# Fused attention and gated feed-forward on one core: first-phase banks, the start of the loop and the last block's outputs rearranged

## The chip, the cores and the metric

The kernel runs on 1 core of one Trainium2 chip. The metric is the device time of one execution in microseconds, as the median of several runs. Every run also reports the span of the core (some 1.8 us less than the time) and the mean clock granted to TensorE. A difference of 2% would count as faster or slower.

## The reference

```python
def mab(q, kv):
    s = scale * (q @ kv.transpose(0, 2, 1))
    a = softmax(s)
    return a @ kv
h = mab(I, x)            # 32 inducing points look at 12416 tokens, 4 batches
x = mab(x, h)            # every token looks at the 32 results
out = (relu(x @ w_gate) * (x @ w_val)) @ w_out      # 49664 tokens, 128 -> 1536 -> 128
```

## The kernel before

Batch 0 has a first phase of its own: cast x, transpose it on TensorE, scores `s1`, exp `p1`, denominators `z1`, and `hT`, the 32 results. The products `hgv` of `hT` with the weights follow in three parts of 512 columns. Then comes the loop that fills the rest of the time. A unit of it is: TensorE forms a gate (two banks of 512) and a value (one tile of two banks), ScalarE takes the relu of the gate, VectorE multiplies the relu with the value into `gv`, and TensorE contracts `gv` with `wo`. The kernel splits PSUM, the memory that TensorE's results go to, into eight banks (3 + 2 x 2 + 1): a ring `g` of three, two two-bank tiles `v`, one bank `o`.

```python
def bank(tag, name, shape=None, dtype=FP32):
    return psum.tile(shape or [P, BLK], dtype, tag=tag, bufs={"g": 3, "v": 2, "o": 1}[tag], name=name)
...
# first phase, batch 0
z1_ps = bank("v", "z1_ps", [P, 2 * BLK])
z1a, z1 = z1_ps[:, 0 : 8 * M], z1_ps[:, BLK : BLK + M]
s1_ps = bank("v", "s1_ps", [P, 2, 2 * TPB, 2 * M])      # scores: one tile of two banks
...
        ps = s1_ps[:, j % 2, :, 0:M]
        for t in range(t0, t1):
            nc.tensor.matmul(ps[:, t - t0, :], xTs(xT, t, 1), indT, start=True, stop=True)
        nc.scalar.activation(out=p1[...], in_=ps[...], func=AF.Exp, scale=sm_scale)
...
# start of the loop: all three parts of hgv first
ps = hgv_pe(hT, 0)
for a in (0, BLK // 2):
    nc.vector.tensor_copy(out=hgv[:, a : a + BLK // 2], in_=ps[:, a : a + BLK // 2])
ps = bank("v", "hgv_ps", [P, 2 * BLK])
for k in (1, 2):
    hgv_pe(hT, k, ps[:, (k - 1) * BLK : k * BLK])
nc.vector.tensor_copy(out=hgv[:, BLK : 2 * BLK], in_=ps[:, 0:BLK])
nc.scalar.copy(out=hgv[:, 2 * BLK : DFF], in_=ps[:, BLK : 2 * BLK])
...
# the last block, its evacuation
for a in (0, h):                                          # h = 2 of 4 token tiles
    nc.vector.tensor_tensor(out=osb[:, a : a + h, :], in0=c["ps"][:, a : a + h, :],
                            in1=zz[0][...], op=ALU.mult)
    nc.sync.dma_start(out=ov[...], in_=osb[:, a : a + h, :])
```

A slot is the place of one unit in the loop. In the first ten slots two filler matmuls a slot keep TensorE busy (`idle`).

The softmax here doesn't subtract the row's maximum and nothing guards it: scores larger than these inputs give would overflow.

## Time and profile before

| | before |
|---|---|
| time, median of 3 runs | 710.46 us (709.27 to 711.6) |
| span of the profiled run | 709.0 us |
| VectorE busy | 678.9 us (96%) |
| ScalarE busy | 675.3 us (95%) |
| first product of the loop | 28.65 us |
| seventh product instruction (the first unit is split in two) | 36.23 us |
| end of the last product | 704.17 us |

Two engines are busy nearly all the time, so the page shows the bound, but not what the ends cost. For that one reads the timeline, line by line: start, length, engine, source line, operation, output and inputs, how many instructions are merged in the line, and in brackets how long the engine was idle before it and what ended the idle time. The prediction below shows these lines.

### The profile page before, as it was taken

How to read it: one execution, taken by the hardware profiler on the slowest of the kernel's cores; microseconds unless marked ns; L12 is line 12 of the kernel's file. 1: busy time of each engine (PE TensorE's matmuls, PEld its weight loads, DVE VectorE, ACT ScalarE, POOL GpSimd, SP SyncE). 2: the span in 40 equal slices, each digit the busy share in tenths (PEclk: the TensorE clock that was granted, in tenths of full speed). 3: DMA queues.
4: the chain of work that ended last, by engine and by line, in shares of the span. 5: the costliest groups of instructions: out<-in, count | busy, mean ns of one | idle time of the engine just before them, and what ended most of it. 6: DMA issues, size and time to landing. Idle time of an engine off the chain costs nothing.

```text
span 709.0 us, 14077 instructions
## 1 busy us (share of the span) xinstructions
PE 637.9 (90%) x4626; PEld 186.0 (26%) x4626; DVE 678.9 (96%) x621; ACT 675.3 (95%) x1382; POOL 350.5 (49%) x646
## 2 busy tenths in 40 slices
PE   6899999999998999999998899999999898888997
PEld 5322222222222222222222222222222222222224
DVE  4599999999999999999999999999999999999997
ACT  5699999999999999999999999999999999999995
POOL 3661637535176546355256362852616443534543
PEclk9999999999999999999999999999999999999999
DMA  8657865431247867523139677653223132231222
GB/s 342 216 129 163 171 178 152 119 82 61 74 145 152 203 167 199 133 82 91 46 107 197 166 175 172 160 124 76 68 67 94 50 90 56 79 89 49 71 58 89
DMA packets 142346, 87.58 MB, mean 124 GB/s; under 512 B 117152, under 2 KB 125632, under 8 KB 139968
## 3 DMA queue, kind: packets, MB, share of 16 engines
q1 hardware_dynamic: 142272, 86.68, 47.2%
q8 instruction: 36, 0.59, 0.4%
q14 instruction: 38, 0.31, 0.1%
HBM read 27.80 MB, written 25.43 MB: 75 GB/s over the span
## 4 chain that ended last, share of the span: by engine, by line
ACT 32%; PE 29%; issue 17%; DVE 14%; DMA 6%; POOL 1%; SPq 1%; ACTq 0%; DVEq 0%
ACT g L961 23%; DVE gv L966 13%; PE o_ps L662 13%; PE v_ps L864 9%; ACT oT L668 5%; PE g_ps L864 4%; DMA gv<-in_x_dram 2%; ACT p2q L195 2%; DMA x<-in_moe_w_val_dram 1%; ACT p1T L527 1%; DMA out_dram<-osb 1%; DMA x<-in_x_dram 1%; PE h_ps L579 1%; POOL osb L679 0%; PE idle_ps L263 0%
## 5 line engine op out<-in xcount | busy, mean ns | idle before, releaser
L966 DVE TENSOR_TENSOR gv<-g,v_ps 128x1024 f16<-128x1024 f16 (+1 forms) x578 | 658.0, 1210 | 9.4 <-PE g_ps L864 5.9
L961 ACT ACTIVATE g<-g_ps 128x512 f16<-128x512 f32 x1164 | 604.0, 618 | 12.3 <-PE g_ps L864 8.5
L662 PE MATMUL o_ps<-gv,wo 128*128 128x512 f16 x1128 | 352.5, 384 | 43.9 <-ACT oT L668 43.9
L679 POOL TENSOR_SCALAR osb<-o,z2i 128x128 f32<-128x128 f16 x380 | 165.9, 453 | 276.0 <-DMA o<-oT 273.9
L864 PE MATMUL g_ps<-p,hgv 32*128 32x512 f16 x1152 | 284.4, 380 | 2.6 <-ACT g L961 1.9
L864 PE MATMUL v_ps<-p,hgv 32*128 32x512 f16 x1152 | 224.2, 384 | 9.5 <-DVE gv L966 7.9
L864 PEld LDWEIGHTS <-hgv 32*128 32x128 f16 x2400 | 69.5, 91 | 269.3 <-issue 264.7
L662 PEld LDWEIGHTS <-wo 128*128 128x128 f16 x1176 | 80.9, 97 | 211.8 <-issue 195.4
L435 POOL TENSOR_TENSOR z2i<-zt,minus 128x16 f32<-128x16 f32 (+3 forms) x31 | 73.2, 2366 | 0.3
L668 ACT CAST oT<-o_ps 128x512 f16<-128x512 f32 (+1 forms) x98 | 58.4, 596 | 0.0
L496 POOL CAST x<-x 128x2048 f16<-128x2048 f32 x18 | 34.0, 1890 | 18.3 <-DMA x<-in_x_dram 18.3
L428 POOL TENSOR_TENSOR zt<-zt 128x32 f32<-128x32 f32 (+5 forms) x124 | 35.1, 283 | 9.7
L428 POOL TENSOR_TENSOR zt<-p2T 128x256 f32<-128x256 f16 (+3 forms) x31 | 17.4, 563 | 25.9 <-DMA p2T<-p 15.2
L270 DVE COPY xT<-xT_ps 128x1024 f16<-128x1024 f16 (+1 forms) x13 | 8.4, 650 | 10.0 <-PE xT_ps L269 9.2
L269 PE MATMUL xT_ps<-eye,x 128*128 128x128 f16 x97 | 9.0, 242 | 5.5 <-POOL x L281 4.8
L282 ACT CAST x<-gv 128x512 f16<-128x512 f32 (+1 forms) x12 | 7.2, 597 | 6.9 <-DMA gv<-in_x_dram 6.9
L195 ACT ACTIVATE p2q<-s_ps 128x512 f16<-128x512 f32 x22 | 13.4, 610 | 0.0
L281 POOL CAST x<-gv 128x512 f16<-128x512 f32 (+1 forms) x12 | 7.2, 598 | 10.2 <-DMA gv<-in_x_dram 10.1
L527 ACT ACTIVATE p1T<-s1T_ps 128x512 f16<-128x512 f32 x18 | 11.1, 616 | 0.0
L179 PE MATMUL s_ps<-xT,hT 128*32 128x512 f16 x108 | 10.8, 392 | 0.2
L601 POOL TENSOR_TENSOR hp<-hp,hq 128x129 f32<-128x129 f32 (+1 forms) x18 | 8.3, 461 | 2.8 <-ACT hq L600 2.8
L966 DVE TENSOR_TENSOR gvr<-g,v_ps 128x512 f16<-128x512 f16 x12 | 8.0, 684 | 1.7 <-PE g_ps L864 1.7
(93 smaller groups left out, 159.1 us busy)
## 6 DMA issues: line engine op xcount, KB each, us to landing
out_dram<-osb SPq DMA_DIRECT2D x95, 256.0 KB, 2.2
x<-in_x_dram SPq DMA_DIRECT2D x18, 1024.0 KB, 6.0
gv<-in_x_dram SPq DMA_DIRECT2D x11, 512.0 KB, 7.5
p<-p2q SPq DMA_DIRECT2D x88, 64.0 KB, 2.0
o<-oT SPq DMA_TRANSPOSE x98, 2.3
x<-in_moe_w_out_dram SPq DMA_DIRECT2D x1, 768.0 KB, 9.2
gv<-in_x_dram SPq DMA_DIRECT2D x2, 256.0 KB, 10.5
x<-in_moe_w_gate_dram SPq DMA_DIRECT2D x1, 512.0 KB, 9.0
```

The costliest lines, as they stand in the source:

```text
L179: nc.tensor.matmul(ps[32 * r : 32 * r + 32, :], hT[:, 0:M], xTs(xT, blocks[r] * TPB, TPB), start=True, stop=True,)
L195: nc.scalar.activation(out=p2q, in_=ps, func=AF.Exp, scale=sm_scale)
L428: nc.gpsimd.tensor_tensor(out=dst, in0=v[:, :, :, 0:m], in1=v[:, :, :, m : 2 * m], op=ALU.add)
L435: nc.gpsimd.tensor_tensor(out=z2i, in0=v[:, :, :, 0], in1=minus1[:, 0 : n * g].rearrange("p (n g) -> p n g", n=n), op=ALU.pow,)
L496: nc.gpsimd.tensor_copy(out=s["x16"][:, t0:t1, :], in_=s["x32", q])
L527: nc.scalar.activation(out=p1T, in_=ps, func=AF.Exp, scale=sm_scale)
L662: nc.tensor.matmul(c["ps"][:, 0:w], wo[:, i, :], gv(i), start=(i == 0), stop=(i == NFF - 1))
L668: nc.scalar.copy(out=oT[:, 0:w], in_=c["ps"][:, 0:w])
L679: nc.gpsimd.tensor_scalar(out=osb[:, t, :], in0=o16[:, t, :], scalar1=zz, scalar2=zz, op0=ALU.mult, op1=ALU.mult,)
L864: nc.tensor.matmul(ps[:, cols], hgv[:, s * P : (s + 1) * P], p2, start=True, stop=True)
L961: nc.scalar.activation(out=g16[:, k * BLK : (k + 1) * BLK], in_=ps, func=AF.Relu)
L966: nc.vector.tensor_tensor(out=ready["dst"][:, a : a + w], in0=ready["g16"][:, a : a + w], in1=ready["v"][:, a : a + w], op=ALU.mult,)
```

## The change

Three intentions. In the first phase the scores of each part take a bank of the ring, so that a tile of two banks is free for the fillers, and the denominators are summed ahead of `hT`. The second and third part of `hgv` become jobs inside the loop, after units 1 and 4, so the loop starts with the first part only; two score jobs of batch 0 move to later slots. The last block's outputs take two banks of the gate ring (384 and 128 columns), scaled by VectorE and ScalarE at once and stored from two queues.

```diff
-    z1_ps = bank("v", "z1_ps", [P, 2 * BLK])
-    z1a, z1 = z1_ps[:, 0 : 8 * M], z1_ps[:, BLK : BLK + M]
-    s1_ps = bank("v", "s1_ps", [P, 2, 2 * TPB, 2 * M])
+    z1a_ps = bank("v", "z1a_ps", [P, 2 * BLK])
+    z1a, idle_ps = z1a_ps[:, 0 : 8 * M], z1a_ps[:, BLK : 2 * BLK]
+    z1 = bank("v", "z1_ps", [P, M])
...
-            ps = s1_ps[:, j % 2, :, 0:M]
+            ps = bank("g", "s1_ps", [P, 8, M])
...
-    ps = bank("v", "hgv_ps", [P, 2 * BLK])
-    for k in (1, 2):
-        hgv_pe(hT, k, ps[:, (k - 1) * BLK : k * BLK])
-    nc.vector.tensor_copy(out=hgv[:, BLK : 2 * BLK], in_=ps[:, 0:BLK])
-    nc.scalar.copy(out=hgv[:, 2 * BLK : DFF], in_=ps[:, BLK : 2 * BLK])
+    idle(idle_ps, 3, xT[0][:, 0:4, :].rearrange("p t c -> p (t c)"))
...
+    ev_hgv(0, 1, 1, 1)          # TensorE, then ScalarE one slot later
+    ev_hgv(0, 2, 4, 4)
...
-                    ev_s2_quad(b, qd, a + 4, a + 8)
+                    ev_s2_quad(b, qd, a + (4 if a else 12), a + (8 if a else 18))
-                ev_s2(b, (b, 1), (2, 3, 2, 3), 5, 8)
+                ev_s2(b, (b, 1), (2, 3, 2, 3), 7, 8)
...
-                ps = bank("o", "o_ps")
+                c["ps"] = bank("g" if last else "o", "o_ps", [P, n, P])      # n = 3 if last
+                if last:
+                    c["ps1"] = bank("g", "o_ps", [P, 1, P])
...
-                for a in (0, h):
-                    nc.vector.tensor_tensor(... half ...);  nc.sync.dma_start(... half ...)
+                nc.vector.tensor_tensor(out=osb[:, 0:n, :], in0=c["ps"], in1=zz[0][...], op=ALU.mult)
+                nc.sync.dma_start(out=ov[...][:, t0 : t0 + n, :], in_=osb[:, 0:n, :])
+                nc.scalar.activation(out=osb1[:, 0, :], in_=c["ps1"][:, 0, :], func=AF.Copy, scale=zz[0][:, n, :])
+                nc.scalar.dma_start(out=ov[...][:, t0 + n : t0 + TPB, :], in_=osb1)
...
-                        job(steps, evac, ([1, 3, 3, 3, 3] if k == 0 else [0] + [4] * 8,) * 2)
+                        job(steps, evac, ([1, 3, 3, 3, 3] if k == 0 else [5] * 8,) * 2)
```

More of the change, by code (lines that the diff above doesn't have):

```diff
@@ L307 @@
                 )
+            end = j == n_parts + 2
+            for t in range(n if j - 3 >= n_big else 0):
+                first, last = j - 3 == n_big and t == 0, end and t == n - 1
+                nc.tensor.matmul(z1, ones16, p1[:, t, :], start=first, stop=last)
             for t in range(n):
-                first, last = j == 3 and t == 0, j == n_parts + 2 and t == n - 1
-                if j - 3 >= n_big:
-                    nc.tensor.matmul(
-                        z1, ones16, p1[:, t, :], start=j - 3 == n_big and t == 0, stop=last
-                    )
+                first, last = j == 3 and t == 0, end and t == n - 1
                 nc.tensor.matmul(hT_ps, x16[:, t0 + t, :], p1[:, t, :], start=first, stop=last)
@@ L319 @@
         if j == n_parts:
-            idle_ps = bank("g", "idle_ps")
             z1s = st([P, M], FP32, "z1s", 1)
@@ L456, in job, with ev_hgv, pe @@
         jobs.append(dict(steps=steps, evac=evac, counts=counts))
+    def ev_hgv(b, k, first, last):
+        def pe(at):
+            ps = hgv_pe(state[b]["hT"], k)
+            post[at + 1].append(lambda: hgv_evac(state[b]["hgv"], ps, k))
+        fill(first, last, pe)
+    ev_hgv(0, 1, 1, 1)
+    ev_hgv(0, 2, 4, 4)
     for b in range(B):
@@ L641, in act @@
                 for k in range(3):
-                    def mk(at, k=k):
-                        ps = hgv_pe(s["hT"], k)
-                        post[at + 1].append(lambda: hgv_evac(s["hgv"], ps, k))
-                    fill(at + 2, at + 9 + 3 * k, mk)
+                    ev_hgv(b, k, at + 2, at + 9 + 3 * k)
             post[at + 1].append(act)
@@ L719, in step @@
             if i == 0:
-                ps = bank("o", "o_ps")
-                nc.tensor.matmul(ps, zero16, wo[0:1, 0:TPB, :], start=True, stop=False)
-                c["ps"] = ps.rearrange("p (t c) -> p t c", t=TPB)
+                n = TPB - 1 if last else TPB
+                c["ps"] = bank("g" if last else "o", "o_ps", [P, n, P])
+                nc.tensor.matmul(c["ps"], zero16, wo[0:1, 0:n, :], start=True, stop=False)
+                if last:
+                    c["ps1"] = bank("g", "o_ps", [P, 1, P])
             for t in range(TPB):
+                alone = last and t == TPB - 1
                 nc.tensor.matmul(
-                    c["ps"][:, t, :],
+                    c["ps1"][:, 0, :] if alone else c["ps"][:, t, :],
                     gv(i)[:, t * P : (t + 1) * P],
                     wo[:, i, :],
-                    start=False,
-                    stop=(i == NFF - 1 and t == TPB - 1),
+                    start=alone and i == 0,
+                    stop=i == NFF - 1 and (alone or t == c["ps"].shape[1] - 1),
                 )
@@ L735, in evac @@
             if last:
-                h = TPB // 2
-                for a in (0, h):
-                    nc.vector.tensor_tensor(
-                        out=osb[:, a : a + h, :],
-                        in0=c["ps"][:, a : a + h, :],
-                        in1=zz[0][:, a : a + h, :].broadcast_to([P, h, P]),
-                        op=ALU.mult,
-                    )
-                    nc.sync.dma_start(
-                        out=ov[key[0]][:, t0 + a : t0 + a + h, :], in_=osb[:, a : a + h, :]
-                    )
+                n = TPB - 1
+                nc.vector.tensor_tensor(
+                    out=osb[:, 0:n, :],
+                    in0=c["ps"],
+                    in1=zz[0][:, 0:n, :].broadcast_to([P, n, P]),
+                    op=ALU.mult,
+                )
+                nc.sync.dma_start(out=ov[key[0]][:, t0 : t0 + n, :], in_=osb[:, 0:n, :])
+                osb1 = st([P, 1, P], FP32, "osb1", 1)
+                nc.scalar.activation(
+                    out=osb1[:, 0, :], in_=c["ps1"][:, 0, :], func=AF.Copy, scale=zz[0][:, n, :]
+                )
+                nc.scalar.dma_start(out=ov[key[0]][:, t0 + n : t0 + TPB, :], in_=osb1)
                 return
```

## The prediction

That a smaller idle gap of TensorE makes the full clock likelier rests on the one stretch at 0.50 in the trace before (29.79 to 33.20 us), after that gap. That a second queue is worth one issue at most rests on issues of 0.33 to 0.39 us. For the 0.15 us of the wider last store no working is given; the page of the kernel before has 1.7 us from issue to landing for stores of 128 KB and 2.2 for 256 KB.

> **What bounds the kernel now.** I read the busy shares first, then the costliest groups, then the timeline of the two ends, because the diff only touches the ends.
>
> From the page of the kernel before (engine busy times; then group: engine, operation, tile, shapes, count | busy us, mean ns | idle before):
>
> ```profile
> PE 637.9 (90%) x4626; PEld 186.0 (26%) x4626; DVE 678.9 (96%) x621; ACT 675.3 (95%) x1382; POOL 350.5 (49%) x646
> ...
> L966 DVE TENSOR_TENSOR gv<-g,v_ps 128x1024 f16<-128x1024 f16 (+1 forms) x578 | 658.0, 1210 | 9.4 <-PE g_ps L864 5.9
> L961 ACT ACTIVATE g<-g_ps 128x512 f16<-128x512 f32 x1164 | 604.0, 618 | 12.3 <-PE g_ps L864 8.5
> ```
>
> VectorE's product gate times value is 658 of 709 us and sits idle only 9.4 us in all. ScalarE (relu 604, plus chain copies, plus exps) is almost as full. So the long middle is a VectorE/ScalarE bound with nothing to give: a change that leaves the instructions of the loop alone can win only before the loop is at full pace and after its last product. The timeline of the start:
>
> ```profile
> 27.47 0.59 ACT L339 CAST hgv<-hgv_ps 128x512 f16<-128x512 f32 x1 [1.40 <-DVE hgv L338]
> 27.95 3.05 ACT L961 ACTIVATE g<-g_ps 128x512 f16<-128x512 f32 x6
> 28.61 0.37 PE L864 MATMUL g_ps<-p,hgv 32*128 32x512 f16 x1 [1.36 <-ACT g L961]
> 28.65 1.29 DVE L966 TENSOR_TENSOR gv<-g,v_ps 128x512 f16<-128x512 f16 x2 [1.21 <-POOL wo L885]
> 30.16 1.22 DVE L966 TENSOR_TENSOR gv<-g,v_ps 128x1024 f16<-128x1024 f16 x1 [0.23 <-PE v_ps L864]
> 31.74 1.22 DVE L966 TENSOR_TENSOR gv<-g,v_ps 128x1024 f16<-128x1024 f16 x1 [0.35 <-PE v_ps L864]
> 33.25 1.22 DVE L966 TENSOR_TENSOR gv<-g,v_ps 128x1024 f16<-128x1024 f16 x1 [0.29 <-PE v_ps L864]
> 34.76 1.22 DVE L966 TENSOR_TENSOR gv<-g,v_ps 128x1024 f16<-128x1024 f16 x1 [0.29 <-ACT p2q L195]
> 36.23 20.71 DVE L966 TENSOR_TENSOR gv<-g,v_ps 128x1024 f16<-128x1024 f16 x18 [0.25 <-ACT p L190]
> ```
>
> ScalarE's first relu waits behind its copy of the last third of hgv, which waits for VectorE's copy of the second third. TensorE, whose three gate banks are full, idles 1.36 us at 28.61. Then five products start 1.5 us apart (30.16, 31.74, 33.25, 34.76, 36.23) where the full pace is 20.71/18 = 1.15. The stretches show why (columns: stretch, its length, busy us and count of PE, PEld, DVE, ACT, POOL, then the granted TensorE clock, DMA share, GB/s):
>
> ```profile
> 29.00:30.00 1.00, 1.00 (x7) 0.23 (x8) 0.93 (x2) 1.00 (x4) 0.77 (x4) 0.89 0.61 188
> 30.00:31.00 1.00, 1.00 (x9) 0.16 (x6) 0.84 (x1) 1.00 (x3) 0.84 (x3) 0.50 1.02 426
> 31.00:32.00 1.00, 1.00 (x7) 0.19 (x6) 0.65 (x2) 0.42 (x2) 1.00 (x1) 0.50 0.78 328
> 32.00:33.00 1.00, 1.00 (x6) 0.11 (x4) 0.96 (x1) 0.67 (x2) 0.22 (x2) 0.50 0.06 16
> 33.00:34.00 1.00, 1.00 (x11) 0.28 (x8) 0.75 (x1) 0.90 (x2) 1.00 (x1) 0.90 0.00 0
> ```
>
> After the idle gap the clock falls to half for about 3.4 us (0.22 us of the first row, three whole rows, 0.2 us of the last), TensorE is busy all of it, and products wait for v_ps. The end:
>
> ```profile
> 701.90 0.39 PE L864 MATMUL v_ps<-p,hgv 32*128 32x512 f16 x2 [0.58 <-DVE gv L966]
> ...
> 702.44 2.85 PE L724 MATMUL o_ps<-wo,gv 128*128 128x128 f16 x48
> 705.38 0.76 DVE L738 TENSOR_TENSOR osb<-o_ps,zz 128x256 f32<-128x256 f32 x2 [1.21 <-issue]
> 705.84 0.81 SPq L744 DMA_DIRECT2D out_dram<-osb  x2
> ```
>
> The last product ends at 704.17 (the chain of waits: 703.58 + 0.60), but the 48 output matmuls could begin only when the single output bank had been copied away (ScalarE's copy, 701.49 + 0.59), so TensorE runs until 702.44 + 2.85 = 705.29. Then two VectorE halves in a row and two stores, the second issued at 706.3 (the groups of the output tensor), landing some 1.7 us later.
>
> [...] The trace's issues cost 0.33 to 0.39 us against 1.7 us to landing, so a second queue is worth one issue at most. [...] The trace gives 420 ns for 256 columns and 691 ns for a 512-column cast, so about 1.06 ns per column.
>
> **The change, part by part.**
>
> *End of the first phase.* The 32-column scores no longer share one two-bank tile; each takes a bank of the ring of three. Before, the score matmuls of 22.40 waited for ScalarE's exp of the part before (end 22.34), and the two exps after it stand at 22.75 and 23.42, 0.67 us apart, because score and exp alternate. After, the instruction order shows no ScalarE wait on those matmuls: they can go at about 22.05, the next exps at about 22.35 and 23.05. The softmax denominators are also summed ahead of hT, so the reciprocal (356 ns) partly hides. Gain **about 0.4 us** at hT.
>
> *Head of the loop.* The copies of the second and third parts of hgv leave the path and become ScalarE jobs after units 1 and 4. VectorE loses one copy (0.69 us); ScalarE gains one. The first relu now waits only for the first gate matmuls: hgv's first part is there at about 26.1, three filler matmuls (0.65 us at 0.216 each) end at 26.35, gates at about 26.45, relu 26.85 to 27.4, first product about 27.45; less the 0.4 above, **27.05 instead of 28.65, 1.6 us earlier**. On the way to full pace the new order carries two ScalarE copies (0.5 us each in a back-to-back stream) but two exps (0.6 each) move from units 4 to 6 to units 8 to 13, where ScalarE's relus run ahead (20 in 9.93 us, 0.99 a unit, against VectorE's 1.15). If the clock stays full, I walk units 0 to 5 at ScalarE's pace: relus of units 0, 1, copy, 2, 3, 4, copy, 5 are 12 x 0.51 + 2 x 0.5 = 7.1 us from 26.85 - 0.4 = 26.45, so the sixth product starts near 33.5 to 34.2 instead of 36.23: **2.0 to 2.7**, less some 0.3 when the moved exps come due: 2.0. If the clock still drops (0.36 us lost in each of 3 to 4 units) it is about 0.9. TensorE's 1.36 us gap shrinks to a few tenths, so I give the full clock 70%: 0.7 x 2.0 + 0.3 x 0.9 = **1.7 us**.
>
> *The tail.* With two gate banks, free once unit 11's relus have been read (about 701.1), 20 of the 48 matmuls go before the last values, 28 after. The 20 take 20 x 0.059 = 1.2 us, so the last v_ps moves from 701.90 to about 702.5 and is complete by about 702.9, when VectorE wants it (its last two halves begin at about 702.95): roughly no loss, 0.15 us at worst. Matmuls of units 9 and 10 fill the time to 704.1; after the last product at 704.17 only four are left, so TensorE ends near 704.65 instead of 705.29: 0.65. VectorE then scales 384 columns in 420 + 128 x 1.06 = 556 ns instead of 760; ScalarE's 128 columns (about 0.3) and its store lie beside it. The last issue falls at about 705.25 instead of 706.3: 1.05, less 0.15 since the last store is 192 KB and not 128. Gain **0.9 us**.
>
> *Sum:* 1.7 + 0.9 = 2.6 us. 710.46 - 2.6 = **707.9 us**.
>
> **Rivals.** (a) *ScalarE takes the head's gain back.* It is nearly as full as VectorE and gets a copy more. By its own account it starts 1.4 us earlier and carries 1.0 more copies, so the head would give only about 0.5 plus the 1.0 us of stalls it had between 31 and 34. For: the chain of waits passes through ScalarE for 32% of the span, VectorE 14%. Against: its relus take 0.51 back to back, 591 us for all 1164, and 0.99 a unit early on. Total gain then 1.5 to 2, time about 708.7. (b) *The clock drops all the same*[...]: the head gives 0.9, time 708.7. (c) *The last v_ps comes late* behind the 20 matmuls, the product waits 0.3 to 0.5, and a first use of ScalarE's queue costs something: tail gain 0.4, time 708.4. (d) *Everything works and the clock stays full*: 2.4 + 1.0, time 707.0. A slower kernel would need the moved exp of the quad, the gate ring shared by scores and transposes, or a late z to stall the middle; the needs for them lie at unit 12 and later and the first phase waits for its loads anyway (x casts of ScalarE waited 6.9 us for them), so I see no such stall.
>
> **Range and chances.** The rivals span 707 to 709; the three runs before spread over 2.3 us (709.27 to 711.6), so I take 706.3 to 709.6. A 2% change is 14 us, far beyond both ends together: faster 0.01, same 0.98, slower 0.01.
>
> **What would show it.** First product near 27.0 and sixth near 34; granted clock 1.0 between 28 and 34 (step right) or 0.50 for about 3.4 us somewhere there (rival b); exps of the last two parts moved forward by 0.4; VectorE idle in the loop still 8 to 9 us (if it grew by 1 to 2, rival a); TensorE's end within 0.5 us of the last product; the two stores issued within 0.4 us of each other. The prediction is wrong if the products in the middle lose more than 1 us to new waits, or if the first phase's loads end later.

## The result, and the profile after

The changed kernel took 708.58 us in the median (708.34 to 709.58, 4 runs), the kernel before 710.53 (709.27 to 711.6, 4 runs). The ratio is 0.9976, with a 95% interval of 0.9957 to 0.9995: by the 2% measure the same, in fact 2 us faster. The span of the profiled run is 706.6 us.

The page of the changed kernel, the same lines as before:

```profile
PE 637.6 (90%) x4629; PEld 186.5 (26%) x4629; DVE 677.7 (96%) x619; ACT 676.1 (96%) x1384; POOL 350.4 (50%) x646
...
L971 DVE TENSOR_TENSOR gv<-g,v_ps 128x1024 f16<-128x1024 f16 (+1 forms) x578 | 657.5, 1209 | 9.9 <-PE g_ps L869 6.0
L966 ACT ACTIVATE g<-g_ps 128x512 f16<-128x512 f32 x1164 | 604.2, 618 | 11.9 <-PE g_ps L869 8.4
```

The loop has the same work, and VectorE's idle time before its products is 9.9 us where it was 9.4. That looks harmless, but the idle time before the first seven products fell from 2.62 to 1.65 us (the sums of their brackets in the two timelines), so something came in elsewhere. The start, VectorE's timeline of the changed kernel:

```profile
26.80 1.28 DVE L971 TENSOR_TENSOR gv<-g,v_ps 128x512 f16<-128x512 f16 x2 [0.98 <-ACT g L966]
28.76 9.21 DVE L971 TENSOR_TENSOR gv<-g,v_ps 128x1024 f16<-128x1024 f16 x8 [0.67 <-ACT hgv L170]
38.18 4.87 DVE L971 TENSOR_TENSOR gv<-g,v_ps 128x1024 f16<-128x1024 f16 x4 [0.21 <-PE g_ps L869]
```

The first product starts at 26.80 and not 28.65, and from 28.76 on eight products run at 9.21/8 = 1.15 us. The slow five, 1.5 us apart, are gone. ScalarE's timeline shows the order that makes this possible, two relus per unit at once and the copies between them:

```profile
26.12 2.06 ACT L966 ACTIVATE g<-g_ps 128x512 f16<-128x512 f32 x4 [0.67 <-PE v_ps L869]
28.05 0.62 ACT L170 CAST hgv<-hgv_ps 128x512 f16<-128x512 f32 x1
28.55 3.07 ACT L966 ACTIVATE g<-g_ps 128x512 f16<-128x512 f32 x6
31.47 0.62 ACT L170 CAST hgv<-hgv_ps 128x512 f16<-128x512 f32 x1
```

And two of the stretches in which the clock was 0.50 before (last three columns: granted clock, DMA share, GB/s):

```profile
30.00:31.00 1.00, 0.90 (x9) 0.38 (x8) 1.00 (x1) 1.00 (x4) 0.92 (x2) 1.00 1.04 442
31.00:32.00 1.00, 1.00 (x11) 0.32 (x7) 1.00 (x2) 1.00 (x4) 0.92 (x2) 1.00 0.14 49
```

The end of the changed kernel, from its timeline:

```profile
700.42 0.39 PE L869 MATMUL v_ps<-p,hgv 32*128 32x512 f16 x2
...
701.28 1.28 DVE L971 TENSOR_TENSOR gv<-g,v_ps 128x512 f16<-128x512 f16 x2 [0.36 <-issue]
...
702.62 0.40 PE L727 MATMUL o_ps<-wo,gv 128*128 128x128 f16 x4 [0.20 <-DVE gv L971]
703.05 0.56 DVE L740 TENSOR_TENSOR osb<-o_ps,zz 128x384 f32<-128x384 f32 x1 [0.49 <-issue]
703.11 0.37 ACT L748 ACTIVATE osb<-o_ps,zz 128x128 f32<-128x128 f32 x1 [3.08 <-PE o_ps L727]
703.51 0.41 ACTq L751 DMA_DIRECT2D out_dram<-osb  x1
703.64 0.33 SPq L746 DMA_DIRECT2D out_dram<-osb  x1
```

From the end of the last product to the end of the span it is now 4.00 us (706.57 - 702.56) where it was 4.87 (709.04 - 704.17). But look at the second line. The last values are complete at 700.42 + 0.39 = 700.81, before the previous product ends (700.92), and yet the last one starts at 701.28, after 0.36 us of idle time that the profile can only call "issue".

The clearest view is the product's start in one kernel less its start in the other, along the loop (worked out from the records of both traces):

```
product instruction     0      2      4      6      9     10     72     87    147    207    537    587    589
before, us          28.65  30.16  33.25  36.23  39.63  40.76 112.03 129.65 198.37 267.31 644.95 701.76 703.49
after - before      -1.84  -1.41  -2.23  -2.91  -2.88  -2.58  -2.58  -2.46  -2.45  -2.17  -2.05  -2.05  -1.61
```

The start wins 2.91 us. Then 1.30 us are given back in steps: 0.30 at product 10, some 0.5 in three small steps in the middle, 0.44 at the last unit. The end wins 0.87. So 2.91 - 1.30 + 0.87 = 2.48, the difference of the spans (709.04 - 706.57 = 2.47). (The medians are only 1.95 apart: the profiled run of the kernel before took 710.82 us, more than its median, and that of the changed kernel 708.34, less.) Two questions are left: what in the start did it, and what takes the 1.30 back.

### The profile page after: what moved, and what is told of

It reads as the page before. It is cut to its first block, busy times and chain, and to the rows that moved or that the text cites. A ratio compares the mean times of both kernels' runs of the same rounds, so it can differ in the third digit from the quotient of the medians. Undisturbed runs are those within 1.5% of the kernel's fastest.

```text
span 706.6 us, 14082 instructions
## 1 busy us (share of the span) xinstructions
PE 637.6 (90%) x4629; PEld 186.5 (26%) x4629; DVE 677.7 (96%) x619; ACT 676.1 (96%) x1384; POOL 350.4 (50%) x646
```

## The experiments

Theories. **Parts:** the start wins by three things, the score banks, the copies off the path and the clock; the end wins by the early matmuls. **Numbering:** the losses in the middle and at the end come from where a pause of VectorE, tied to its instruction number, falls. **Rivals:** the losses come from ScalarE's added copy (the prediction's first rival), or the one at the end from the 20 matmuls ahead of the last values (its third).

What suggested the numbering: VectorE waits for TensorE in an instruction of its own and then starts the product. The traces record 605 such waits (EVENT_SEMAPHORE) each. With VectorE idle, the product starts about 0.045 us after its wait has passed in nearly all of both traces (0.043 to 0.052, once 0.120 in the kernel before), except for seven in the changed kernel, where it is 0.395 to 0.457. Counting VectorE's records from 0, these are numbers 63, 191, 319, 447, 831, 1087 and 1215, all of them 63 plus a multiple of 128. In the kernel before, the same numbers fall on the wait instruction or on a product with time to spare, since the change removed one VectorE copy ahead of the loop.

The kernel before was run 27 times more, and its runs fall into groups by mean granted clock. By an estimate from the stretch of 3.41 us at 0.50 in the trace before, a mean of 0.998 over 709 us is what one such stretch gives (3.4 x 0.5 / 709 = 0.0024), and 0.995 what two give. On three chips the kernel before at full clock took 709.58, 709.65 and 709.65 us in the mean, so figures can be compared to about 0.1 us.

| mean clock of the run | runs of the kernel before | median us |
|---|---|---|
| 0.999 or 1.000 | 9 | 709.67 |
| 0.997 or 0.998 | 11 | 710.57 |
| 0.994 or 0.995 | 7 | 711.17 |

All results below, with the mean of the runs at 0.999 or more as a second measure that the clock doesn't blur:

| kernel | median us | ratio to before | at full clock: runs, mean us |
|---|---|---|---|
| before | 710.57, 709.80, 710.79 | 1 | 9 of 27, 709.63 |
| changed kernel, again | 708.54 | 0.9974 | 8 of 9 with the first four, 708.53 |
| head only | 709.06 | 0.9986 | 3 of 5, 708.98 |
| tail only | 710.07 | 0.9994 | 0 of 5 |
| changed, plus memset | 707.81 | 0.9963 | 5 of 5, 707.77 |
| before, plus memset | 711.81 | 1.0015 | 1 of 5, 710.15 |
| before, gap filled | 709.74 | 0.9994 | 3 of 5, 709.65 |
| changed, old score banks | 709.65 | 0.9986 | 2 of 5, 708.92 |
| changed, last values earlier | 708.32 | 0.9972 | 5 of 5, 708.30 |
| changed, hgv copy on VectorE | 708.27 | 0.9968 | 2 of 5, 707.86 |
| changed, one queue | 708.63 | 0.9972 | 5 of 5, 708.66 |
| memset and earlier values | 707.85 | 0.9963 | 4 of 5, 707.85 |
| hgv copy and earlier values | 707.68 | 0.9959 | 5 of 5, 707.69 |

### The changed kernel again

No edit; a control on the chip of the first call.

> Control: the changed kernel itself, for comparison on this chip. Every theory: ratio 0.9975 to the kernel before (708.6 against 710.5). If the clock explains the spread of its runs, a run whose mean granted clock is 0.998 takes about 1 us more than one at 1.000 (in the four runs so far: 709.58 at 0.998 against 708.34 to 708.72).

708.54 us (708.42 to 708.67), ratio 0.9974 (0.9961 to 0.9986). The result repeats. In its trace the late products stand at the same numbers, with idle times within 0.02 us of the first trace's. All five runs had the full clock, so of the changed kernel's nine runs only one hadn't, and it took 709.58.

### The head alone and the tail alone

Head only: the changed kernel with the last block's code and step counts of before. Tail only: the kernel before with those of the changed kernel (the last hunks of the diff above).

> The changed kernel with the old tail (one output bank, two VectorE halves, one queue). Theory of the parts: the last product starts about 2.05 us earlier than before and the tail takes its old 4.8 us from the last product's end, so 2.0 us gained (ratio 0.9971), because the 0.43 us that the new tail loses at the last product stays away. Rival, the tail's own gain as predicted (0.9): only 1.7 gained and the changed kernel clearly ahead of this one by 0.8.

Measured 709.06, so 1.5 us under the kernel before and 0.5 over the changed kernel (0.45 at full clock). In its trace the last product ends at 702.26 and the tail takes 4.86, against 702.68 and 4.00 in the changed kernel's trace of the same call: the new tail wins 0.86 and loses 0.42 at the last product. My 2.0 was too high, since it came from a trace of the kernel before with a stretch at half clock, which not all of its runs have; the rival's 0.8 was too high as well.

> The kernel before with the new tail alone. If the 0.36 us idle before the last product comes from the 20 output matmuls put ahead of the last values, it shows here too: tail gain 0.36 to 0.45 us. If it comes from where VectorE's instruction number 1215 falls (a pause of 0.35 us between the wait and the product, seen at numbers 63 plus multiples of 128 in the changed kernel only, where the head has one VectorE instruction less), it doesn't show here, the idle is under 0.1 us and the gain is about 0.8 us (ratio 0.9989).

The time can't decide here: 710.07, ratio 0.9994 with an interval of 0.9981 to 1.0006. All five of its runs had 0.998, and against runs of the kernel before at 0.997 or 0.998 (710.61 in the mean) it is 0.6 ahead. The trace decides: the tail takes 4.00, the last product is number 1216 and starts 0.043 us after its wait, with no idle time, at a cost of 0.08 us against the steady pace. The 20 matmuls ahead of the last values are there in full. So they are not what delays the last product of the changed kernel.

### One more VectorE instruction

```diff
     nc.vector.memset(ones16, 1.0)
+    pad = constp.tile([P, 1], FP32, name="pad")
+    nc.vector.memset(pad, 0.0)          # nobody reads it
```

> The changed kernel with one tiny VectorE memset more at the start, of a tile nobody reads. If the pauses follow the instruction number, the five idle times of VectorE with 0.395 us between wait and product (at 114.7, 188.5, 261.7, 628.2 and 701.3) lose 0.35 us each or vanish, no product starts more than 0.06 us after its wait while VectorE is idle, and the time falls by 0.4 to 1.0 us against the changed kernel (to about 707.9). If the last product waits because of the matmul order, its idle of 0.36 stays and the time stays within 0.2 us.

707.81 us (707.59 to 708.0), 0.73 less than the changed kernel, by an instruction that does nothing. Its last five products, from VectorE's timeline:

```profile
697.30 4.76 DVE L973 TENSOR_TENSOR gv<-g,v_ps 128x1024 f16<-128x1024 f16 x5
702.55 0.56 DVE L742 TENSOR_TENSOR osb<-o_ps,zz 128x384 f32<-128x384 f32 x1 [0.49 <-issue]
```

They run together in one line without a gap. Product 76 in the changed kernel, and the same product with the memset:

```profile
114.74 11.40 DVE L971 TENSOR_TENSOR gv<-g,v_ps 128x1024 f16<-128x1024 f16 x10 [0.69 <-ACT p1T L532]
114.73 10.50 DVE L973 TENSOR_TENSOR gv<-g,v_ps 128x1024 f16<-128x1024 f16 x9 [0.34 <-PE g_ps L871]
```

Along the loop its lead over the kernel before is 2.24 us at product 20 and still 2.20 at product 587; the changed kernel went from 2.58 to 2.05. With the last unit, the loss after product 10 falls from 0.97 to 0.12 us, so 0.85 is won. But this trace's first product also comes 0.34 us later than the changed kernel's (27.14), and that of the other run with the memset 0.52 later. A run with the same head and no memset comes up to 0.35 later (hgv copy and earlier values), so whether the memset delays the start stays open. Of the 0.85 this pair of traces keeps 0.51 (706.57 - 706.05 in span); the medians are 0.73 apart.

The edit on the kernel before is the mirror test.

> The kernel before with the same unread memset. The mirror test: if the pauses follow the instruction number, the shift by one puts number 63 plus multiples of 128 between VectorE's wait and its product here, so products with 0.395 us between wait and start and idle time before them appear, where the kernel before has none, and the time grows by 0.5 to 1.0 us (ratio about 1.001). If the memset helped the changed kernel in another way (as by delaying the start), the time is unchanged or falls.

711.81 us, ratio 1.0015 (1.0001 to 1.0029). Most of its runs had a low clock (0.994 to 0.997), so the time alone would prove little; its one run at full clock took 710.15, half a microsecond over the mean of before at full clock. The trace is clear again. Its lag behind the kernel before is 0.37 us at product 20 and 1.12 at product 587, and late products stand where there were none. Some of them, from the records (number of the VectorE record; us from wait to start; idle us before it):

```
product   before               after                after + memset      before + memset
  76      192  0.043  0.329    191  0.401  0.688    192  0.051  0.338   193  0.044  none
 139      318  0.045  none     317  0.045  none     318  0.045  none    319  0.395  0.310
 140      320  0.043  0.423    319  0.396  0.775    320  0.043  0.421   321  0.044  0.074
 204      448  0.049  none     447  0.395  0.267    448  0.048  none    449  0.287  none
 523     1086  0.084  none    1085  0.086  none    1086  0.084  none   1087  0.395  0.235
 588     1221   -     none    1215  0.396  0.358   1216  0.042  none   1222   -     none
```

Read the column of numbers: wherever a product carries 191, 319, 447, 1087 or 1215, it comes 0.35 us later, whatever kernel and product it is; one number further it doesn't. This settles that the pause follows the number. What the pause is, the trace doesn't say. It records transfers that it calls "instruction" beside those of the program, and of the 38 of 8192 bytes in the changed kernel's span one starts 0.67 to 0.70 us after the start of each of the seven late products (42.53, 115.44, 189.21, 262.45, 483.11, 628.89 and 701.96). Whether they have to do with the pause isn't shown: no run took one away, and each starts when the late product has already begun.

### The clock

The kernel before with fillers in TensorE's idle gap, and nothing else:

```diff
-            for m in unit["mm"][0]:
+            for i, m in enumerate(unit["mm"][0]):
+                if at == 1 and i == 1:
+                    idle(idle_ps, 6, hgv[:, 0:BLK])
                 gate(*m)
```

> The kernel before with six filler matmuls in TensorE's idle 1.36 us at 27.2 to 28.6, between the two gate matmuls of the second unit; nothing else. If the half clock comes from that gap, the granted clock stays 1.0 between 29 and 34 in most runs (mean 0.999 or 1.000 where the kernel before has 0.998 or less in 7 of 9 runs), products 2 to 6 start about 1.15 to 1.2 apart and not 1.5, and the time falls by about 1.0 us to some 709.5, the time of the kernel before in its one run at 1.000. If the products are held by something else, the time stays at 710.5.

VectorE's timeline of that kernel:

```profile
28.69 1.28 DVE L968 TENSOR_TENSOR gv<-g,v_ps 128x512 f16<-128x512 f16 x2 [1.21 <-PE idle_ps L263]
30.16 4.65 DVE L968 TENSOR_TENSOR gv<-g,v_ps 128x1024 f16<-128x1024 f16 x4 [0.18 <-ACT g L963]
35.06 10.52 DVE L968 TENSOR_TENSOR gv<-g,v_ps 128x1024 f16<-128x1024 f16 x9 [0.25 <-ACT p L190]
```

The clock stayed at 1.0, products run at 4.65/4 = 1.16 us, and the seventh product instruction starts at 35.06, 1.17 us ahead of before. That is the clock's share of the 2.91, in this pair of traces, where the clock had dropped in the one and not in the other. The median, 709.74, is close to the forecast 709.5, but the runs of before beside it mostly had the full clock by luck (five of nine), so the ratio is 0.9994 and shows nothing. And two of its own five runs had 0.998: filling this gap makes the drop rarer at most, it doesn't exclude it. That it is rarer isn't shown with five runs. Other traces show why it can't be excluded here: their clock records have stretches of 3.41 us at 0.50 from 20.17 and again from 30.41 (the kernel before with the memset, mean clock of that run 0.995), from 20.44 (old score banks, 0.997) and from 206.24, deep in the loop (hgv copy on VectorE, 0.998). So the drop isn't tied to this gap alone, and its cause stays open.

### The score banks

The changed kernel, with the scores back in their shared tile of two banks:

```diff
+    s1_ps = bank("v", "s1_ps", [P, 2, 2 * TPB, 2 * M])
+    idle_ps = s1_ps[:, 0, :, :].rearrange("p t m -> p (t m)")
-            ps = bank("g", "s1_ps", [P, 8, M])
+            ps = s1_ps[:, j % 2, :, 0:M]
```

(The denominators are back in one tile of two banks with it, to make room; their grouped order stays.)

> The changed kernel with the scores of the first phase back in their shared two-bank tile. If that sharing made score and exp alternate, the last two exps are 0.6 to 0.7 us apart again, hT comes 0.4 to 0.6 us later, and the time is about 0.5 us over the changed kernel (709.0). Rival, the grouped denominators did it: hT comes no later than 24.4 and the time equals the changed kernel's 708.5.

ScalarE's timeline at the end of the first phase, the changed kernel first:

```profile
21.79 0.69 ACT L292 ACTIVATE p<-s_ps 128x256 f16<-128x256 f32 x2 [0.74 <-PE s_ps L290]
22.88 0.28 ACT L292 ACTIVATE p<-s_ps 128x128 f16<-128x128 f32 x1 [0.41 <-PE s_ps L290]
```

And with the old banks:

```profile
22.64 0.38 ACT L293 ACTIVATE p<-s_ps 128x256 f16<-128x256 f32 x1 [1.11 <-PE s_ps L291]
23.44 0.28 ACT L293 ACTIVATE p<-s_ps 128x128 f16<-128x128 f32 x1 [0.42 <-PE s_ps L291]
24.12 0.28 ACT L293 ACTIVATE p<-s_ps 128x128 f16<-128x128 f32 x1 [0.40 <-PE s_ps L291]
```

From the third exp from the end to the last it is 1.48 us with the old banks, 1.09 with the ring (22.88 - 21.79). So the shared tile did make score and exp alternate, and the ring is worth 0.4 us. This trace also had a half clock at 20.4 to 23.9, so the kernel before is the cleaner comparison: 23.42 - 21.96 = 1.46, the same.

```profile
21.96 0.38 ACT L292 ACTIVATE p<-s_ps 128x256 f16<-128x256 f32 x1 [0.76 <-PE s_ps L290]
22.75 0.28 ACT L292 ACTIVATE p<-s_ps 128x128 f16<-128x128 f32 x1 [0.40 <-PE s_ps L290]
23.42 0.28 ACT L292 ACTIVATE p<-s_ps 128x128 f16<-128x128 f32 x1 [0.40 <-PE s_ps L290]
```

The time is 709.65 with three of five runs off the full clock; the two at full clock, 708.79 and 709.05, are 0.4 over the changed kernel's 708.53.

### The last values earlier

```diff
-                        job(steps, evac, ([1, 3, 3, 3, 3] if k == 0 else [5] * 8,) * 2)
+                        job(steps, evac, ([1, 3, 3, 3, 3] if k == 0 else [3, 9],) * 2)
```

> The changed kernel with 12 and 36 output matmuls around the last values, not 20 and 28. VectorE's numbering is unchanged, so the pause at number 1215 stays; but its wait is passed some 0.45 us earlier, so the pause lies beside the product before it and the idle of 0.36 falls under 0.1: 0.4 us gained (708.1). TensorE must still end within 0.6 us of the last product. If neither holds, the last product's delay isn't understood.

708.32 us, 0.22 under the changed kernel where 0.4 was expected. In the trace the values are formed at 700.08, the last product still is number 1215 and starts 0.408 us after its wait, but that now lies beside the product before it: no idle time, and the last product ends at 702.22 (the changed kernel's traces: 702.56 and 702.68). So there are two ways round the pause, another number or an earlier wait. Why the times show only half of it stays open.

### ScalarE's added copy

```diff
+            if (b, k) == (0, 1):
+                post[at + 1].append(lambda: nc.vector.tensor_copy(
+                    out=state[b]["hgv"][:, BLK : 2 * BLK], in_=ps))
+            else:
                 post[at + 1].append(lambda: hgv_evac(state[b]["hgv"], ps, k))
```

> The changed kernel with the copy of the second third of hgv on VectorE, in the 0.67 us in which it waits before the second unit's product. This adds one VectorE instruction, so the numbering shifts as with the memset and the pauses go too: it must be read against the run with the memset (707.8). If ScalarE's two added copies cost the 0.30 us that the product of unit 9 loses (38.18), that product starts with under 0.05 us idle and the time is about 707.5. If ScalarE had room for both, it equals 707.8.

The product of unit 9 is idle 0.21 us before it, as in the changed kernel, and starts no earlier. At full clock (two runs) the kernel takes 707.86, the same as with the memset (707.77); its median of 708.27 holds three runs with a lower clock. So ScalarE had room for the copy, and my theory for the 0.30 us at that product falls. The wait there is for the values: in the changed kernel's trace they are formed at 37.68 to 38.07, 0.3 us after the first output matmul of the loop, which was put ahead of them. That TensorE's order at unit 9 is the cause is argued from one trace, not shown.

### One queue

```diff
-                nc.scalar.dma_start(out=ov[key[0]][:, t0 + n : t0 + TPB, :], in_=osb1)
+                nc.sync.dma_start(out=ov[key[0]][:, t0 + n : t0 + TPB, :], in_=osb1)
```

> The changed kernel with both last stores from the sync queue. The second queue is worth one issue of 0.33 us at most: the wider store is the one that ends last and follows in the order first, so it is issued at about the same time after the last product, and the narrow one 0.33 us after it: 0.1 to 0.3 us slower than the changed kernel (708.7), tail 4.1 to 4.3 us against 4.00 from the last product's end. If the queue matters more[...], 0.5 us or more.

708.63 us against 708.54, and the tail takes 4.03 us against 4.00. Its two issues:

```profile
703.75 0.33 SPq L746 DMA_DIRECT2D out_dram<-osb  x1
704.17 0.38 SPq L751 DMA_DIRECT2D out_dram<-osb  x1
```

The second issue comes 0.42 us after the first, and its narrow store now lands last, at 705.82, 0.21 us after the wide one. But counted from the last product's end that is 3.15 us, where the last store of the changed kernel, the wide one, lands after 3.12. The "one issue of 0.33 us at most" of the expectation was an estimate from the issue of 0.33 us at 703.64 in the changed kernel; measured, the second queue is worth 0.09 us in the medians and 0.03 in the tail, which is within the runs' spread (708.34 to 708.72 at full clock for the changed kernel): the time is at the lower end of what was expected, and the tail, forecast at 4.1 to 4.3, under it.

### Two combinations

> Memset and the 12/36 order together. The last product's wait of 0.36 can be won only once: with the memset 0.08 of idle was left there, so this gains 0.05 to 0.1 us over the memset alone (707.7). If the two were separate causes, it gains 0.3 to 0.4 (707.4).

707.85 us, the memset's 707.81 again: the last product's wait can be won only once.

> VectorE's copy of the second third of hgv and the 12/36 order together, in the changed kernel: the candidate for the best. If the parts add, 707.8 - 0.3 - 0.1 = 707.4.

707.68 us (707.53 to 707.83), the lowest median of all, with no late product at all and full clock in all five runs. It beats the kernel before (ratio 0.9959, 0.9946 to 0.9971) and the changed kernel (by 0.86 us), but not clearly the one with the memset, and the sum of 707.4 was missed, as the copy wins nothing by itself.

## Why the prediction was right or wrong

The time lay in the range, 708.6 against 707.9, and the sum of the parts was 2.6 where 2.0 was measured. The direction and most of the mechanism held.

- **End of the first phase, 0.4 us at hT.** Right: hT comes at 24.12 and not 24.75. Of these 0.63 us the phase's earlier start gives 0.17 (21.79 against 21.96) and the exps 0.37 (1.09 against 1.46); the old banks run gives 0.4.
- **Head of the loop, "the first product about 27.45; less the 0.4 above, 27.05".** It came at 26.80. The seventh product instruction came at 33.3 where "33.5 to 34.2" was forecast, 2.91 us gained where 2.0 to 2.7 was. The walk at ScalarE's pace came near. Of the 1.84 us at the first product 0.63 stand at hT already; the other 1.2 belong to the copies taken off the path, by subtraction only, since no run tested them alone. The 0.3 allowed for the moved exps has a counterpart of the right size, the 0.30 at product 10. The agreement is probably luck: that product waits for the values, and moving a copy away from ScalarE doesn't help it. No run moved the exps alone.
- **The clock.** "I give the full clock 70%" was cautious: eight of nine runs had it. What the step overlooked is the other side: the kernel before has the full clock in a third of its runs too, so the half clock seen in its trace isn't a fixed cost. At full clock on both sides the change is worth 709.63 - 708.53 = 1.1 us; the other 0.9 of the 2.0 between the medians is that the half clock came less often in the changed kernel's runs. Why it did isn't shown.
- **The middle.** "VectorE idle in the loop still 8 to 9 us (if it grew by 1 to 2, rival a)". The lead shrank by 0.53 between products 10 and 587, and it wasn't rival (a): the run with the copy on VectorE takes no less at full clock than the one with the memset, and the memset alone keeps the lead. The step that failed is the unspoken one in "a change that leaves the instructions of the loop alone can win only before the loop is at full pace and after its last product". The change also shifts the numbers of VectorE's instructions in the loop by one, and undoing that alone gains 0.73 us.
- **The tail, "roughly no loss, 0.15 us at worst" for the last values.** In itself right: with the product at number 1216, in the tail only run and the memset run, the loss is 0.08 us. In the changed kernel it is 0.44, since its number is 1215. Rival (c) named a wait of 0.3 to 0.5 at this place, with the wrong cause.
- **The rest of the tail.** TensorE's end 0.46 us after the last product (0.5 forecast), 557 ns for 384 columns (556 forecast), 0.37 us for ScalarE's 128 columns (about 0.3 forecast), stores issued 0.13 us apart, 0.87 us gained from the last product on (0.9 forecast as the whole gain). Right in nearly every term; for the wider last store 0.15 us was allowed, and it took 2.0 us to landing where the 128 KB stores had taken 1.7. ScalarE's queue changed the time by 0.09 us, its issue took 0.41 us and its store landed after 1.8.

So the forecast time was 0.6 to 0.7 us too low. The traces show the sum: the head gave 2.58 us from product 10 on, where 1.7 was forecast (2.0 if the clock stays full); the tail gave 0.87, where 0.9 was; and the middle and the last unit took back 0.53 and 0.44, for which the forecast had no term but the "0.15 us at worst". That the time lies so near the forecast is in part luck: a head better than forecast covered some of what the numbering took.

## What to carry to other kernels

When two kernels differ by a microsecond, plot the start of each repeated instruction in one against the other along the loop: gains and losses then stand as steps at definite places, where totals cancel. Look at the instruction numbers of late starts that the profile calls "issue": here VectorE's stood 128 or a multiple of 128 apart, each product starting about 0.395 us after its wait and not 0.045; one memset ahead of them moved them and won 0.73 us in the medians, and forming the last values 0.34 us earlier (700.08 against 700.42) hid the last one and won 0.22. And sort the runs by granted clock before comparing them; here runs of the kernel before with a mean of 0.999 or 1.000 and with 0.997 or 0.998, which is by estimate one stretch of 3.4 us at half clock, form groups 0.9 us apart (709.67 and 710.57).
